# Two query blocks of an attention in turns, and the numbers by which a planner places the other work

## The chip, the cores and the metric

The kernel runs on one core of a Trainium2 chip. Its time is the device time of one execution in microseconds (us); a kernel is told by the median of its runs. Five engines work side by side, each through its own queue in order: TensorE (PE) multiplies matrices, VectorE (DVE) and ScalarE (ACT) work on whole tiles, SyncE (SP) issues nearly all DMA transfers here, and GpSimd (POOL) does nothing of weight.

## The reference

```python
scores = (1.0 / S) * np.matmul(z, z.transpose(0, 2, 1))      # z: (4, 3072, 64)
attn = np.maximum(scores, 0.0) ** 2
x = u * np.matmul(attn, v)                                   # u, v: (4, 3072, 256)
x_prev = np.concatenate([zeros, x[:, :-1, :]], axis=1)
xk = mu_k * x + (1.0 - mu_k) * x_prev
xr = mu_r * x + (1.0 - mu_r) * x_prev
k = np.maximum(xk @ w_k, 0.0)                                # w_k: (256, 1024)
y = 1.0 / (1.0 + np.exp(-(xr @ w_r))) * (k * k @ w_v)
return (np.maximum(y @ w_in, 0.0) ** 2) @ w_out              # w_in: (256, 2048), w_out: (2048, 256)
```

The weights come as 64-bit numbers. Every product is made of three: each operand is split into a rounded part (hi) and its rest (lo), and hi·hi, lo·hi and hi·lo are added up.

## The kernel before

The program has two parts: the attention (with the conversion of the weights beside it), and then the channel mix and the two-layer network, which the change leaves as they are.

**Steps.** Each of the 4 batches has 6 query blocks of 512; the 24 blocks are numbered n, and ib is a block's number within its batch. A block needs 24 steps, one for each chunk of 128 keys, in 6 groups g of 4 chunks. So there are 576 steps s, and `chunk(s)` says which block, group and chunk a step has. The main loop issues, for each s, first what the planner placed there, then `scores(s + 4)`, then `attend(s)`. `attend` is 6 matmuls (L371 and L372 with the hi part of the squared scores, L375 with their lo part). `scores` has three cases:
- g equal to ib ("diagonal"): two matmuls (L343, L344) into PSUM, relu (L157) and square (L158) on ACT, the hi part by DVE (L350), and one step later the lo part by DVE (L353).
- g above ib ("off"): the same, but ACT makes the hi part in two of three steps (L348), and DVE transposes the squared scores (L314, tile `turn`, two buffers). After 4 chunks the tile is stored to DRAM (L318, `turned`). The table `spread` picks the form: for ib of 2 and above the store's layout is "spread", and the transpose takes longer.
- g below ib ("turned"): the scores are the transposed ones of an earlier block. No matmul: `mixed` is loaded from `turned` (L328 or L330), ACT makes hi (L338) and DVE lo (L339).

So a diagonal or off step has 8 matmuls, a turned one 6. Block 0 of a batch has 4 diagonal and 20 off steps, block 5 has 20 turned and 4 diagonal ones, which come first.

**What else lies in the steps.** Each group of z must be turned (`z_turn` L256, DVE), split (`z_hi` L263 on ACT, `z_lo` L266 on DVE) and each group of v split (`prep_v`: L280 on ACT, L278 on DVE). At a block's end the two halves of the result are multiplied by u (`gate` L380, after `prep_u` L290) and stored (L381). The 64-bit weights are converted in 25 pieces of 8 DVE operations each (L119 to L143; 18 more for rests), `conversions`.

**The planner.** Each such piece of work has a cost, an earliest step e and a due step l. The planner goes through the steps with a running balance of the DVE time that a step leaves (`time_left`), puts the piece that is due first into a step when there is room, and at its due step in any case. Conversions get an even spacing over a list of steps `free`. `place` then puts the loads some steps ahead of their use. `EARLY` is how many steps ahead the transposed scores are loaded.

**Queue and buffers.** SP issues in the order in which the code emits. A v load and a weight load (both L91) use the same pool `raw` of 3 buffers; either waits in SP until DVE and ACT have read the buffer's last content, and all that stands behind it in SP waits too.

Of the kernel before, what the change touches and what calls it, by code (L numbers as in the profile page):

```python
# [7 lines left out]
F32 = mybir.dt.float32  # L8
F32R = mybir.dt.float32r
# [6 lines left out]
P = 128  # L16
Q = 32
T = 512
# [3 lines left out]
def tile_relu2_attention__rwkv_channel_mix__relu2_mlp(  # L22
# [18 lines left out]
    nc = tc.nc  # L41
# [5 lines left out]
    NJ = S // P  # L47
    NB = S // T
    NBLK = B * NB
# [5 lines left out]
    G = 4  # L55
    NG = NJ // G
# [20 lines left out]
    spread = {(i, j): i >= 2 for j in range(NB) for i in range(j)}  # L77
# [114 lines left out]
    def acc_tiles(pool=ps_v):  # L192
        return [pool.tile([P, T], F32, tag=f"v{d}", name=f"v{d}") for d in range(ND)]
# [38 lines left out]
    def attention():  # L232
        with ExitStack() as st:
            zp = st.enter_context(tc.tile_pool(name="zp", bufs=1))
            io = st.enter_context(tc.tile_pool(name="io", bufs=2))
            pools["cv"] = st.enter_context(tc.tile_pool(name="cv", bufs=1))
            ps_a = st.enter_context(tc.tile_pool(name="ps_a", bufs=1, space=PSUM))
            ps_w = st.enter_context(tc.tile_pool(name="ps_s", bufs=4, space=PSUM))
            LEAD = 4
# [3 lines left out]
            def load_turned(t, p, src, engine=nc.sync):  # L243

                engine.dma_start(out=t[p:p + Q].rearrange("q (k r) -> q k r", r=Q),
                                 in_=src.rearrange("(k q) r -> q k r", q=Q))

            def load_z(b, g, engines=(nc.sync, nc.sync)):
                z_raw[b, g] = t = io.tile([DQ, T], F32, tag="zn", name="zn")
                for p, e in zip(range(0, DQ, Q), engines, strict=True):  # L250
                    load_turned(t, p, z[b, g * T:(g + 1) * T, p:p + Q], e)


            def z_turn(b, g):
# [37 lines left out]
            at, acc, ready, staged, late = {}, {}, {}, {}, []  # L292
# [2 lines left out]

            def chunk(s):

                n, jc = divmod(s, NJ)  # L300
                if n % NB == NB - 1:
                    jc = (jc - G) % NJ
                return n, n // NB, n % NB, jc // G, jc % G

# [54 lines left out]

            def attend(s):
                n, b, ib, g, c = chunk(s)
                first, last = s % NJ == 0, s % NJ == NJ - 1
                if first:
                    acc[n] = acc_tiles(ps_a if n % 2 else ps_v)
                hi, lo = at.pop(s)
                vt = vhl[b, g]
                for d in range(ND):
                    ds_ = slice(d * P, (d + 1) * P)  # L370
                    nc.tensor.matmul(acc[n][d], lhsT=vt[:, 0, c, ds_], rhs=hi, start=first, stop=False)  # L371
                    nc.tensor.matmul(acc[n][d], lhsT=vt[:, 1, c, ds_], rhs=hi, start=False, stop=False)  # L372
                for d in range(ND):
                    ds_ = slice(d * P, (d + 1) * P)
                    nc.tensor.matmul(acc[n][d], lhsT=vt[:, 0, c, ds_], rhs=lo, start=False, stop=last)  # L375
# [10 lines left out]
            def at_step(s, f, *a):  # L386
                todo.setdefault(s, []).append((f, a))

            n_steps = NBLK * NJ
            for n in range(NBLK):  # L390
                for d in range(ND):
                    at_step(n * NJ + NJ, gate, n, d)

            freed, taken, EARLY = [], 0, 30
            for n in range(NBLK - 1):
                b, ib = divmod(n, NB)
                for g in range(ib):
                    need, stored = n * NJ + (g + ib // (NB - 1)) * G - LEAD, (b * NB + g) * NJ + ib * G + G - 1 - LEAD
# [28 lines left out]
            def time_left(t):  # L427
                if t >= n_steps:
                    return 0.5
                n, _, ib, g, _ = chunk(t)  # L430
                left = 0.72 if g < ib else 0.85 if g == ib else 0.05 if spread[ib, g] else 0.4
                return left - (0.6 if t % NJ in (LEAD, LEAD + 1) and t > NJ else 0)

            first_of = lambda b, g: b * NB * NJ + G * g
            chains, loads = [], []
            for b in range(B):
                z_chain, v_chain = [], []
                chains += [z_chain, v_chain]
                for g in range(NG):
                    i = g | 1  # L440
                    e = first_of(b - 1, 0) + (i * NJ + (NJ if i < NB - 1 else G)) - LEAD if b else -LEAD
                    l = min(first_of(b, g) if not b else first_of(b, 0) - 3 * (NG - g), first_of(b, g)) - LEAD - 2
                    if b or g > 1:
# [3 lines left out]
                    e = first_of(b - 1, 0) + (NB - 1) * NJ + G * min(g + 2, NG) if b else max(-LEAD + 1, G * g - 8)  # L447
                    l = e + (9 if g == NG - 1 else 3) if b else first_of(b, g) - 3
                    v_chain += [(0.2 + 0.4 * lo, prep_v, (b, g, h, lo), e, l + h * 2 + lo) for h in range(2) for lo in range(2)]
            for n in range(NBLK):  # L450
                for d in range(ND):
                    chains.append([(0.65, prep_u, (n, d), n * NJ + 4, n * NJ + 14 + 4 * d)])
            free = [t for t in range(NJ, n_steps - NJ) if chunk(t + LEAD)[2] < NB - 1 and time_left(t + LEAD) > 0.2]
            total = sum(8 + rests for _, _, rests in conversions)
            k0 = 0
            converting = []
# [21 lines left out]
            def place(load, use, last_use, bufs, ahead):  # L478
                ts = sorted((t, a[:2]) for (f, a), t in when.items() if (f, a[2:]) == use)
                done = sorted(t for (f, a), t in when.items() if (f, a[2:]) == last_use)  # L480
                for i, (t, a) in enumerate(ts):
                    s = max(t - ahead, done[i - bufs] + 1 if i >= bufs else -LEAD, -LEAD)
                    assert s < t or t < 0, (a, s, t)
                    if (load, a) != (load_v, (0, 0)):
                        todo.setdefault(s, []).insert(0, (load, a))

            place(load_z, (z_turn, ()), (z_turn, ()), 2, 8)
            place(load_u, (prep_u, ()), (prep_u, ()), 2, 8)
            place(load_v, (prep_v, (0, 0)), (prep_v, (1, 1)), 3, 8)

            s = n_steps - NJ
# [15 lines left out]

            at_step(2 * NJ, load_mu)
            at_step(3 * NJ, lambda: nc.vector.tensor_scalar(out=om, in0=mu, scalar1=-1.0, scalar2=1.0, op0=ALU.mult, op1=ALU.add))
            for g in range(2):  # L510
                load_z(0, g, (nc.sync, nc.scalar))
            load_v(0, 0)
            for g in range(2):
                z_turn(0, g)
                for first in (True, False):
                    z_hi(0, g, first)
                    z_lo(0, g, first)
            for s in range(-LEAD, n_steps + 1):
                for f, a in todo.pop(s, ()):
                    f(*a)  # L520
# [124 lines left out]
    with tc.manual_schedule():  # L645
        attention()
        channel_mix_and_mlp()
# [29 lines left out]
```

## Time and profile before

| | us |
|---|---|
| median of 3 runs (lowest to highest) | 2620.96 (2620.56 to 2626.17) |
| the profiled execution | 2623.58 |
| its span in the trace | 2621.8 |
| PE, DVE, ACT busy in the span | 2584.5, 1762.7, 1516.5 |
| attention part, to the first change of pace | 0 to about 1003.6 |

The profiled execution lies 2.62 us above the median and 1.78 us above its own span. PE's granted clock over the whole run is 0.998 of full. Line numbers are those of the kernel before; in the changed kernel L343 to L381 stand 4 lines further down (L375 becomes L379, L314 becomes L318), while L91, L256, L263, L266, L278, L280 and L290 stay.

### The profile page before, as it was taken

How to read it: one execution, taken by the hardware profiler on the slowest of the kernel's cores; microseconds unless marked ns; L12 is line 12 of the kernel's file. 1: busy time of each engine (PE TensorE's matmuls, PEld its weight loads, DVE VectorE, ACT ScalarE, POOL GpSimd, SP SyncE). 2: the span in 40 equal slices, each digit the busy share in tenths (PEclk: the TensorE clock that was granted, in tenths of full speed). 3: DMA queues.
4: the chain of work that ended last, by engine and by line, in shares of the span. 5: the costliest groups of instructions: out<-in, count | busy, mean ns of one | idle time of the engine just before them, and what ended most of it. 6: DMA issues, size and time to landing. Idle time of an engine off the chain costs nothing.

```text
span 2621.8 us, 32181 instructions
## 1 busy us (share of the span) xinstructions
PE 2584.5 (99%) x11328; PEld 2128.0 (81%) x11328; DVE 1762.7 (67%) x3074; ACT 1516.5 (58%) x2527; POOL 0.2 (0%) x4
## 2 busy tenths in 40 slices
PE   7999999999999999999999999999999999999998
PEld 5888788878788788888888888888888888888887
DVE  7898898898889886655555555555555555555554
ACT  7766876776687665554455545445444554455544
POOL 0000000000000000000000000000000000000000
PEclk9999999999999999999999999999999999999999
DMA  6667667577767761000000000000000000000000
GB/s 164 177 183 191 186 189 193 170 229 194 187 215 193 197 177 65 17 17 17 17 17 17 17 14 11 17 17 17 13 12 17 17 17 17 17 17 17 17 9 17
DMA packets 275602, 215.51 MB, mean 82 GB/s; under 512 B 185072, under 2 KB 203504, under 8 KB 272368
## 3 DMA queue, kind: packets, MB, share of 16 engines
q1 hardware_dynamic: 273328, 213.06, 30.6%
q8 instruction: 88, 1.44, 0.2%
q10 hardware_dynamic: 2112, 0.39, 0.1%
q14 instruction: 74, 0.61, 0.1%
HBM read 121.13 MB, written 92.27 MB: 81 GB/s over the span
## 4 chain that ended last, share of the span: by engine, by line
PE 91%; DVE 2%; DMA 2%; ACT 2%; issue 1%; SPq 1%; DVEq 0%; ACTq 0%
PE ups L203 32%; PE v L375 8%; PE v L372 8%; PE v L371 8%; PE o L564 7%; PE o L565 7%; PE o L568 7%; PE v L219 3%; PE v L218 3%; PE v L222 3%; PE sps L344 2%; PE sps L343 2%; DMA turned<-turn 1%; DMA xT<-uT 1%; DVE alo L353 1%
## 5 line engine op out<-in xcount | busy, mean ns | idle before, releaser
L157 ACT ACTIVATE a<-ups 128x512 f32<-128x512 f32 x576 | 344.1, 597 | 758.5 <-PE ups L203 742.7
L84 DVE CAST hhi<-a 128x512 fp32r<-128x512 f32 x568 | 241.9, 426 | 620.3 <-ACT a L158 603.0
L158 ACT ACTIVATE a<-a 128x512 f32<-128x512 f32 x912 | 576.8, 632 | 29.1
L203 PE MATMUL ups<-x,win 128*128 128x512 f32 x2304 | 584.7, 389 | 0.5 <-DVE x L84 0.5
L203 PEld LDWEIGHTS ups<-x,win 128*128 128x128 f32 x2304 | 432.4, 188 | 90.7 <-DVE x L84 0.9
L372 PE MATMUL v<-ahi,vhl 128*128 128x512 f32 x1152 | 451.1, 392 | 9.9 <-DVE vhl L278 9.9
L371 PE MATMUL v<-ahi,vhl 128*128 128x512 f32 x1152 | 450.0, 391 | 0.9 <-DVE ahi L350 0.9
L85 DVE TENSOR_TENSOR hlo<-a,hhi 128x512 fp32r<-128x512 f32 x568 | 393.5, 693 | 53.1 <-DVE hhi L84 0.9
L375 PE MATMUL v<-alo,vhl 128*128 128x512 f32 x1152 | 358.4, 392 | 11.5 <-DVE alo L339 5.9
L564 PE MATMUL o<-hhi,wout 128*128 128x512 f32 x768 | 298.8, 389 | 0.0
L565 PE MATMUL o<-hhi,wout 128*128 128x512 f32 x768 | 298.8, 389 | 0.0
L203 PE MATMUL ups<-mixed,wk 128*128 128x512 f32 x1152 | 292.1, 389 | 0.0
L375 PEld LDWEIGHTS v<-alo,vhl 128*128 128x128 f32 x1152 | 215.3, 188 | 64.0 <-DVE alo L353 10.8
L372 PEld LDWEIGHTS v<-ahi,vhl 128*128 128x128 f32 x1152 | 217.3, 189 | 58.5 <-DVE vhl L278 13.2
L371 PEld LDWEIGHTS v<-ahi,vhl 128*128 128x128 f32 x1152 | 217.1, 188 | 46.7 <-issue 1.6
L203 PEld LDWEIGHTS ups<-mixed,wk 128*128 128x128 f32 x1152 | 216.2, 188 | 44.9
L157 ACT ACTIVATE a<-sps 128x512 f32<-128x512 f32 x336 | 199.7, 594 | 89.0 <-PE sps L344 82.5
L568 PE MATMUL o<-hlo,wout 128*128 128x512 f32 x768 | 236.4, 389 | 0.0
L314 DVE STREAM_TRANSPOSE turn<-a 128x512 f32<-128x512 f32 x240 | 206.8, 862 | 29.3 <-ACT a L158 14.0
L353 DVE TENSOR_TENSOR alo<-a,ahi 128x512 fp32r<-128x512 f32 x336 | 220.9, 659 | 0.0
L338 ACT CAST ahi<-mixed 128x512 fp32r<-128x512 f32 x220 | 130.6, 618 | 123.9 <-PE v L372 59.4
L565 PEld LDWEIGHTS o<-hhi,wout 128*128 128x128 f32 x768 | 144.2, 188 | 30.0
(70 smaller groups left out, 2558.5 us busy)
## 6 DMA issues: line engine op xcount, KB each, us to landing
turned<-turn SPq DMA_DIRECT2D x60, 1024.0 KB, 4.8
mixed<-turned SPq DMA_DIRECT2D x220, 256.0 KB, 5.1
raw<-in_v_dram SPq DMA_DIRECT2D x24, 512.0 KB, 4.4
u<-in_u_dram SPq DMA_DIRECT2D x192, 64.0 KB, 4.2
xT<-uT SPq DMA_DIRECT2D x48, 256.0 KB, 3.8
out_dram<-y SPq DMA_DIRECT2D x94, 128.0 KB, 2.9
x<-xT SPq DMA_DIRECT2D x20, 513.0 KB, 3.8
zz<-turned SPq DMA_DIRECT2D x20, 256.0 KB, 4.6
```

Source lines behind the costliest of these rows:

```text
L84: nc.vector.tensor_copy(hi, src)
L85: nc.vector.tensor_tensor(out=lo, in0=src, in1=hi, op=ALU.subtract)
L157: nc.scalar.activation(out=a, in_=ps, func=AF.Relu, scale=scale)
L158: nc.scalar.activation(out=a, in_=a, func=AF.Square)
L203: nc.tensor.matmul(ps, lhsT=lhs(h, c, f), rhs=rhs[:, m, c, :], start=k == 0, stop=k == 3 * ND - 1)
L353: finish(lambda: nc.vector.tensor_tensor(out=lo, in0=a, in1=hi, op=ALU.subtract))
L371: nc.tensor.matmul(acc[n][d], lhsT=vt[:, 0, c, ds_], rhs=hi, start=first, stop=False)
L372: nc.tensor.matmul(acc[n][d], lhsT=vt[:, 1, c, ds_], rhs=hi, start=False, stop=False)
L375: nc.tensor.matmul(acc[n][d], lhsT=vt[:, 0, c, ds_], rhs=lo, start=False, stop=last)
L564: nc.tensor.matmul(acc_o[n][d], lhsT=w[:, 0, c, ds_], rhs=hi, start=f == 0, stop=False)
L565: nc.tensor.matmul(acc_o[n][d], lhsT=w[:, 1, c, ds_], rhs=hi, start=False, stop=False)
L568: nc.tensor.matmul(acc_o[n][d], lhsT=w[:, 0, c, ds_], rhs=lo, start=False, stop=f == NF2 - 1)
```

## The change

Blocks 0 and 1 of the first batch are worked in turns, a group of the one and a group of the other (list `order`); all later blocks keep their order. `first`, `last`, the gates and all due steps are rewritten with `pos` and `end`. The planner's numbers change: what a step leaves, where conversions may stand (from block 2 on in place of block 1, filter 0.1 in place of 0.2), earliest and due steps of v and z, and how far ahead u, z and the transposed scores are loaded. Only the first z group is loaded and split ahead of the loop, and ten matmuls of zeros are issued ahead of the first scores.

```diff
+            order = [(0, 0)] + [(n, g) for g in range(1, NG) for n in range(2)] + [(1, 0)]
+            order += [(n, (g - (n % NB == NB - 1)) % NG) for n in range(2, NBLK) for g in range(NG)]
+            pos = {ng: i * G for i, ng in enumerate(order)}
+            end = [max(pos[n, g] for g in range(NG)) + G for n in range(NBLK)]
...
-                n, jc = divmod(s, NJ)
-                if n % NB == NB - 1:
-                    jc = (jc - G) % NJ
-                return n, n // NB, n % NB, jc // G, jc % G
+                n, g = order[s // G]
+                return n, n // NB, n % NB, g, s % G
...
-            freed, taken, EARLY = [], 0, 30
+            freed, taken, EARLY = [], 0, 36
...
-                left = 0.72 if g < ib else 0.85 if g == ib else 0.05 if spread[ib, g] else 0.4
-                return left - (0.6 if t % NJ in (LEAD, LEAD + 1) and t > NJ else 0)
+                left = 0.72 if g < ib else 0.8 if g == ib else 0 if spread[ib, g] else 0.15
+                return left - (0.6 if t - LEAD in end or t - LEAD - 1 in end else 0)
...
-            free = [t for t in range(NJ, n_steps - NJ) if chunk(t + LEAD)[2] < NB - 1 and time_left(t + LEAD) > 0.2]
+            free = [t for t in range(2 * NJ, n_steps - NJ) if chunk(t + LEAD)[2] < NB - 1 and time_left(t + LEAD) > 0.1]
...
-            place(load_z, (z_turn, ()), (z_turn, ()), 2, 8)
-            place(load_u, (prep_u, ()), (prep_u, ()), 2, 8)
+            place(load_z, (z_turn, ()), (z_turn, ()), 2, 12)
+            place(load_u, (prep_u, ()), (prep_u, ()), 2, 14)
...
-            for g in range(2):
-                load_z(0, g, (nc.sync, nc.scalar))
+            load_z(0, 0, (nc.sync, nc.scalar))
             load_v(0, 0)
-            for g in range(2):
-                z_turn(0, g)
-                for first in (True, False):
-                    z_hi(0, g, first)
-                    z_lo(0, g, first)
+            load_z(0, 1, (nc.scalar, nc.scalar))
+
+            t = io.tile([P, T], F32R, tag="ahi", name="zeros", bufs=LEAD + 1)
+            nc.vector.memset(t.bitcast(F32), 0.0)
+            ps = ps_w.tile([P, T], F32, tag="w", name="warm")
+            for i in range(10):
+                nc.tensor.matmul(ps, lhsT=t[:, 0:P], rhs=t, start=True, stop=True)
+            z_turn(0, 0)
+            for first in (True, False):
+                z_hi(0, 0, first)
+                z_lo(0, 0, first)
```

What the planner makes of it is read from the order of the instructions on each engine. Three places matter.

**The start, DVE.** Before, both z groups (`zT` from `zn`, `zz`) are made ahead of the first hi part (`ahi`):

```order
L256 STREAM_TRANSPOSE zT_124<-zn_116 64x512
L266 TENSOR_TENSOR zz_126<-zT_124,zz_126 64x512 x2
L256 STREAM_TRANSPOSE zT_131<-zn_119 64x512
L266 TENSOR_TENSOR zz_126<-zT_131,zz_126 64x512 x2
L256 STREAM_TRANSPOSE zT_145<-zn_142 64x512
L350 CAST ahi_153<-a_150 128x512
L350 CAST ahi_168<-a_165 128x512
L353 TENSOR_TENSOR alo_154<-a_150,ahi_153 128x512
L278 TENSOR_TENSOR vhl_158<-raw_122,vhl_158 128x512
```

Now the second z group comes behind the first hi part, and its last rest (the second `zz` from `zT_158`) only behind the third hi part and the second v rest (`vhl`):

```order
L266 TENSOR_TENSOR zz_139<-zT_137,zz_139 64x512 x2
L354 CAST ahi_155<-a_152 128x512
L256 STREAM_TRANSPOSE zT_158<-zn_121 64x512
L266 TENSOR_TENSOR zz_139<-zT_158,zz_139 64x512
L278 TENSOR_TENSOR vhl_163<-raw_119,vhl_163 128x512
L354 CAST ahi_172<-a_169 128x512
L357 TENSOR_TENSOR alo_156<-a_152,ahi_155 128x512
L354 CAST ahi_186<-a_183 128x512
L357 TENSOR_TENSOR alo_173<-a_169,ahi_172 128x512
L278 TENSOR_TENSOR vhl_163<-raw_119,vhl_163 128x512
L266 TENSOR_TENSOR zz_139<-zT_158,zz_139 64x512
```

That last row is what the fifth pair of score matmuls waits for, and in PE's queue the first `attend` stands behind that pair, before and now.

**The start of the fourth batch, SP.** Here `turned0_1` is the store of the first transposed group of the batch, `raw` a v or weight load, `u` the load of u in four parts. Before, only the two stores of the last block's result (`xT2`) and a v load stand ahead of it:

```order
L91 DMA raw_7384<-in_v_dram 128x4x256
L422 DMA w_out32_79<-m_6934 128x2x256
L91 DMA raw_7469<-in_v_dram 128x4x256
L381 DMA xT2_82<-uT_7192 128x512
L381 DMA xT2_82<-uT_7220 128x512
L318 DMA turned0_1_84<-turn_7484 128x4x512
L330 DMA mixed_7550<-turned0_1_84 32x4x512
```

Now a weight load, then a v load that takes over a buffer, and a u load stand ahead of it:

```order
L91 DMA raw_7434<-in_moe2_w_out_dram 128x2x512
L245 DMA u_7452<-in_u_dram 32x16x32 x4
L385 DMA xT2_82<-uT_7313 128x512
L385 DMA xT2_82<-uT_7363 128x512
L91 DMA raw_7519<-in_v_dram 128x4x256
L245 DMA u_7538<-in_u_dram 32x16x32 x4
L322 DMA turned0_1_84<-turn_7490 128x4x512
```

The v load `raw_7519` waits for DVE's last read of `raw_7415`. On DVE of the changed kernel that read (the first L278 here) stands two rows ahead of the first transpose of the third group, which takes the buffer of `turned0_1`'s store:

```order
L318 STREAM_TRANSPOSE turn_7576<-a_7626 128x16x32
L357 TENSOR_TENSOR alo_7610<-a_7606,ahi_7609 128x512
L278 TENSOR_TENSOR vhl_7565<-raw_7415,vhl_7565 128x512
L128 SCALAR_TENSOR_TENSOR e_7114<-raw_6775,e_7114 128x512
L318 STREAM_TRANSPOSE turn_7652<-a_7646 128x16x32
L357 TENSOR_TENSOR alo_7630<-a_7626,ahi_7629 128x512
```

So the store can only be issued after that L278, and the transpose two rows later waits until it has landed. The third batch has the same sequence now (v load, u load, store), and in the second batch a weight load alone stands in the store's way.

**The last steps of a spread stretch, DVE** (block 14, chunks 20 to 23). Before, one conversion (L143) and no turn of u stand in this place:

```order
L143 TENSOR_TENSOR m_6049<-m_6049,e_5981 128x512
L350 CAST ahi_6223<-a_6220 128x512
L314 STREAM_TRANSPOSE turn_6226<-a_6220 128x16x32
L353 TENSOR_TENSOR alo_6204<-a_6200,ahi_6203 128x512
L314 STREAM_TRANSPOSE turn_6226<-a_6239 128x16x32
L353 TENSOR_TENSOR alo_6224<-a_6220,ahi_6223 128x512
L314 STREAM_TRANSPOSE turn_6226<-a_6256 128x16x32
```

Now two conversions (L119, L122) and a turn of u (L290) stand there:

```order
L119 TENSOR_SCALAR e_6215<-raw_5886 128x512
L354 CAST ahi_6223<-a_6220 128x512
L318 STREAM_TRANSPOSE turn_6226<-a_6220 128x16x32
L357 TENSOR_TENSOR alo_6204<-a_6200,ahi_6203 128x512
L290 STREAM_TRANSPOSE uT_6236<-u_5978 128x512
L122 TENSOR_SCALAR e_6215<-e_6215 128x512
L318 STREAM_TRANSPOSE turn_6226<-a_6242 128x16x32
L357 TENSOR_TENSOR alo_6224<-a_6220,ahi_6223 128x512
```

Over the 12 spread steps of this block the order has 3 conversions and no turn of u before, 7 conversions and 2 turns of u now. Over all spread off steps it has 13 conversions before and 51 now; beside the other off steps 55 and 56, beside diagonal steps 53 and 50, beside turned steps 97 and 61.

## Rows read from the trace of the kernel before

**Rows 1.** The page's busy times: engine, busy us, share of the span, instructions.

```profile
PE 2584.5 (99%) x11328; PEld 2128.0 (81%) x11328; DVE 1762.7 (67%) x3074; ACT 1516.5 (58%) x2527; POOL 0.2 (0%) x4
```

**Rows 2.** Windows: stretch, us, busy us (count) of PE, PEld, DVE, ACT, POOL; clock, DMA.

```profile
0.00:111.80 111.80, 94.09 (x376) 73.23 (x377) 88.57 (x154) 85.53 (x146) 0.20 (x4) 0.97 0.63 172
264.60:310.00 45.40, 43.36 (x186) 34.02 (x186) 38.05 (x69) 36.70 (x63) 0.00 (x0) 1.00 0.67 202
504.00:550.70 46.70, 43.34 (x185) 34.07 (x184) 37.98 (x69) 35.68 (x61) 0.00 (x0) 1.00 0.68 202
747.20:788.90 41.70, 41.70 (x185) 34.53 (x185) 37.95 (x69) 35.52 (x61) 0.00 (x0) 1.00 0.75 227
```

**Rows 3.** The chain that ended last, a stretch in the network: start, us, what.

```profile
1020.33 2.72 PE ups L203 x12
```

**Rows 4.** Timeline of DVE, the start: start, us, instruction, count [idle before <-releaser].

```profile
3.82 0.70 DVE L256 STREAM_TRANSPOSE zT<-zn 64x512 f32<-64x512 f32 x1 [3.82 <-DMA zn<-in_z_dram]
```

**Rows 5.** Timeline of ACT, the start.

```profile
7.44 1.26 ACT L263 CAST zz<-zT 64x512 fp32r<-64x512 f32 x2 [1.62 <-DVE zT L256]
8.72 0.60 ACT L157 ACTIVATE a<-sps 128x512 f32<-128x512 f32 x1
9.35 0.63 ACT L158 ACTIVATE a<-a 128x512 f32<-128x512 f32 x1
```

**Rows 6.** Timeline of PE, the start.

```profile
6.76 0.77 PE L344 MATMUL sps<-zz 128*128 128x512 f32 x1
7.32 0.63 PE L343 MATMUL sps<-zz 128*128 128x512 f32 x1
7.75 0.63 PE L344 MATMUL sps<-zz 128*128 128x512 f32 x1
...
18.05 0.47 PE L371 MATMUL v<-ahi,vhl 128*128 128x512 f32 x1
```

**Rows 7.** Timeline of SP, first block of the third batch.

```profile
516.94 0.37 SPq L91 DMA_DIRECT2D raw<-in_v_dram  x1
...
518.38 0.46 SPq L318 DMA_DIRECT2D turned<-turn  x1
525.24 0.32 SPq L330 DMA_DIRECT2D mixed<-turned  x1
525.60 2.03 SPq L245 DMA_DIRECT2D u<-in_u_dram  x4
```

**Rows 8.** Timeline of DVE there: the third and fourth transposed groups begin.

```profile
525.32 0.71 DVE L314 STREAM_TRANSPOSE turn<-a 128x512 f32<-128x512 f32 x1 [5.08 <-DMA turned<-turn]
...
534.17 0.71 DVE L314 STREAM_TRANSPOSE turn<-a 128x512 f32<-128x512 f32 x1 [2.12 <-DMA turned<-turn]
```

**Rows 9.** The page's DMA issues: count, KB each, median us from issue to landing.

```profile
turned<-turn SPq DMA_DIRECT2D x60, 1024.0 KB, 4.8
```

**Rows 10.** Timeline of DVE, the end of block 14's spread stretch.

```profile
621.47 0.71 DVE L143 TENSOR_TENSOR m<-m,e 128x512 f32<-128x512 f32 x1
622.07 0.45 DVE L350 CAST ahi<-a 128x512 fp32r<-128x512 f32 x1
622.40 1.12 DVE L314 STREAM_TRANSPOSE turn<-a 128x512 f32<-128x512 f32 x1
623.43 0.67 DVE L353 TENSOR_TENSOR alo<-a,ahi 128x512 fp32r<-128x512 f32 x1
624.00 1.12 DVE L314 STREAM_TRANSPOSE turn<-a 128x512 f32<-128x512 f32 x1
...
628.52 1.27 DVE L353 TENSOR_TENSOR alo<-a,ahi 128x512 fp32r<-128x512 f32 x2
```

**Rows 11.** Timeline of PE there: the lo products of block 14's last chunk but one.

```profile
630.03 0.62 PE L375 MATMUL v<-alo,vhl 128*128 128x512 f32 x2
```

**Rows 12.** Waits of PE from 112 to 1003 us: engine, line, waited for, us, times, longest.

```profile
PE v L375 <- DVE alo L339: 5.9, 6, 1.9
```

More of the change, by code (lines that the diff above doesn't have):

```diff
@@ L363, in attend @@
                 n, b, ib, g, c = chunk(s)
-                first, last = s % NJ == 0, s % NJ == NJ - 1
+                first, last = n not in acc, s + 1 == end[n]
                 if first:
@@ L391, in attention @@
                 for d in range(ND):
-                    at_step(n * NJ + NJ, gate, n, d)
-            freed, taken, EARLY = [], 0, 30
+                    at_step(end[n], gate, n, d)
+            freed, taken, EARLY = [], 0, 36
             for n in range(NBLK - 1):
@@ L397, in attention @@
                 for g in range(ib):
-                    need, stored = n * NJ + (g + ib // (NB - 1)) * G - LEAD, (b * NB + g) * NJ + ib * G + G - 1 - LEAD
+                    need, stored = pos[n, g] - LEAD, pos[b * NB + g, ib] + G - 1 - LEAD
                     s = max(need - EARLY, stored + 1, freed[-4] if len(freed) > 3 else 0, taken)
@@ L430, in time_left @@
                 n, _, ib, g, _ = chunk(t)
-                left = 0.72 if g < ib else 0.85 if g == ib else 0.05 if spread[ib, g] else 0.4
-                return left - (0.6 if t % NJ in (LEAD, LEAD + 1) and t > NJ else 0)
-            first_of = lambda b, g: b * NB * NJ + G * g
-            chains, loads = [], []
+                left = 0.72 if g < ib else 0.8 if g == ib else 0 if spread[ib, g] else 0.15
+                return left - (0.6 if t - LEAD in end or t - LEAD - 1 in end else 0)
+            chains = []
             for b in range(B):
                 z_chain, v_chain = [], []
-                chains += [z_chain, v_chain]
+                chains += [v_chain, z_chain]
+                n0 = b * NB
                 for g in range(NG):
[L440 to L443, printed above, removed]
+                    if b:
+                        n = n0 - NB + (g | 1)
+                        e, l = (end[n] if g < NB - 2 else pos[n, NB - 1] + G) - LEAD, end[n0 - 1] - 3 * (NG - g) - LEAD - 2
+                    else:
+                        e, l = max(1 - LEAD, pos[0, g] - LEAD - 9), pos[0, g] - LEAD - (3 if g > 1 else 1)
+                    if b or g:
                         z_chain += [(0.65, z_turn, (b, g), e, l - 5), (0, z_hi, (b, g, True), e, l - 4),
@@ L446, in attention @@
                                     (0.6, z_lo, (b, g, False), e, l)]
-                    e = first_of(b - 1, 0) + (NB - 1) * NJ + G * min(g + 2, NG) if b else max(-LEAD + 1, G * g - 8)
-                    l = e + (9 if g == NG - 1 else 3) if b else first_of(b, g) - 3
-                    v_chain += [(0.2 + 0.4 * lo, prep_v, (b, g, h, lo), e, l + h * 2 + lo) for h in range(2) for lo in range(2)]
+                    if b:
+                        e = end[n0 - 1] - G * max(NG - 2 - g, 0)
+                        l = e + (10 if g == NG - 1 else 4)
+                    else:
+                        e, l = max(1 - LEAD, pos[0, g] - 10), pos[0, g] - 5
+                    v_chain += [(0.2 + 0.4 * lo, prep_v, (b, g, h, lo), e, l + h * 3 + lo) for h in range(2) for lo in range(2)]
             for n in range(NBLK):
                 for d in range(ND):
-                    chains.append([(0.65, prep_u, (n, d), n * NJ + 4, n * NJ + 14 + 4 * d)])
-            free = [t for t in range(NJ, n_steps - NJ) if chunk(t + LEAD)[2] < NB - 1 and time_left(t + LEAD) > 0.2]
+                    e = (end[n - 1] if n else 0) + 3
+                    chains.append([(0.65, prep_u, (n, d), e, min(e + 10 + 4 * d, end[n] - 4 + d))])
+            free = [t for t in range(2 * NJ, n_steps - NJ) if chunk(t + LEAD)[2] < NB - 1 and time_left(t + LEAD) > 0.1]
             total = sum(8 + rests for _, _, rests in conversions)
@@ L483, in place @@
                     assert s < t or t < 0, (a, s, t)
-                    if (load, a) != (load_v, (0, 0)):
+                    if (load, a) != (load_v, (0, 0)) and (load, a) != (load_z, (0, 1)):
                         todo.setdefault(s, []).insert(0, (load, a))
-            place(load_z, (z_turn, ()), (z_turn, ()), 2, 8)
-            place(load_u, (prep_u, ()), (prep_u, ()), 2, 8)
+            place(load_z, (z_turn, ()), (z_turn, ()), 2, 12)
+            place(load_u, (prep_u, ()), (prep_u, ()), 2, 14)
             place(load_v, (prep_v, (0, 0)), (prep_v, (1, 1)), 3, 8)
```

## The prediction

> **What bounds the kernel now.** First the page: PE is busy in 99% of the span [rows 1], so a change can win only what PE still waits, and lose by making it wait more. What a matmul costs when nothing waits is read from the chain: twelve in 2.72 us, 0.2267 us each [rows 3]. A diagonal or off step (8 matmuls) is then 1.81 us, a turned one (6) 1.36 us. The windows show where PE falls behind that pace. The first two blocks have 376 matmuls, 85.2 us at full pace, and take 111.8 us: 26.6 us are lost [rows 2]. The first block of each later batch has 185 or 186 matmuls and takes 41.7 us in the fourth batch, 45.4 in the second, 46.7 in the third: 3.7 and 5.0 us lost, and none [rows 2]. In the rest of the attention PE's longest list of waits is for lo parts of turned steps, 5.9 us in 6 waits [rows 12]. The network behind it runs at pace, isn't touched, and counts at nothing.
>
> **The start and the two blocks in turns.** Before, attend of the second chunk begins at 18.05, with 18 matmuls done [rows 6]. I follow the chain by hand with the new order. The second score product ends at 7.53 (6.76 + 0.77) [rows 6]. ACT's relu, which stood behind the two casts of the second z group until 8.72 [rows 5], can go then: relu 0.62, square 0.63, so DVE's hi part is made at 9.1. Now the second z group begins: turn to 9.8 (0.70 [rows 4]), two casts to 11.1 (1.26 [rows 5]), one v cast to 11.6 (taken as the CASTs). Relu and square of the second chunk end at 12.9, and of the third, with another v cast between, at 14.6. DVE then has a hi part (0.33), a lo part (0.57), a v rest (0.6) and the last z rest (0.7): 16.8. The fifth pair of score products and the first attend follow at the pace of the first ones, 0.43 us from start to start [rows 6], eight of them: 20.2, and the next pair brings attend of the second chunk to 20.6, 2.6 us later than before. From there 376 - 18 = 358 matmuls are left, and z and v groups are wanted only every eighth step in place of every fourth, so I let PE run at pace: 81.2 us, end at 101.8 in place of 111.8. That is **-10.0 us**. Bounds: -7, since ACT has 85.5 us of work in these blocks [rows 2] against PE's 85.2 and may cost some 3 us, and -12.5, if the start is no later than before.
>
> The ten products of zeros cost at most 4.3 us at 0.43. They need only the memset, and DVE is idle until 3.82 and PE until the first score product behind it [rows 4]; without that cover a late memset would delay the scores by what is left of the 4.3. I take 0. No row shows PE busy from the start, so what the clock does then isn't seen: the rows show 0.43 us from start to start for the early scores, twice the 0.2267, that is 1.2 GHz in place of 2.4, after an idle start.
>
> The Trainium skill, page "TensorE: Matmul & The Clock Gate", section "Part 1: The HAM clock gate (the "warmup" mystery)", says that the array is throttled by default and that activity releases it. By that rule the zeros might release the first scores: two products at 0.23 in place of 0.43 would bring the relu some 0.4 to 0.9 us forward, and the sum would be -10.9 in place of -10.0.
>
> I keep 0, since the following wait of PE (from the fourth score pair to 16.8) gives the clock time to fall again.
>
> **The starts of the later batches.** Here a store holds DVE. In the third batch the v load goes out at 516.94, the store of the first transposed group at 518.38, it has landed at 525.24 (6.86 us) [rows 7], and only then DVE goes on with the third group, after 5.08 us idle; the fourth waits 2.12 us more [rows 8]. Of these 7.2 us PE loses 5.0 [rows 2], so 2.2 us of a stall are covered by the lead of four steps. In the changed order of the third and the fourth batch the v load waits for DVE's last v rest, and behind it in SP stand the u load and the store; on DVE there is one operation (0.60) until the transpose that needs the store's buffer. Counted from that rest: v load 0.42 (516.94 and the next issue), u load 2.1 (2.03 and a gap), landing 6.86 [rows 7], less 0.6: DVE stands 8.8 us. The fourth group waits less than before, because the u load is already through: I take 0.7. PE loses 8.8 + 0.7 - 2.2 = 7.3 us, twice, 14.6 against 5.0 + 0. In the second batch only a weight load stands between: 0.42 + 6.86 - 0.33 + 0.7 - 2.2 = 5.5 against 3.7. Together **+11.4 us**. Low bound: all landings at the median of 4.8 us [rows 9] and no second stall, 4.5 + 4.5 + 2.7 against 8.7: +3. High bound: the second stall at 2.1 again, 8.7 + 8.7 + 6.9 against 8.7: +15.6.
>
> **Conversions beside spread steps.** The new order puts 51 conversion operations beside spread steps, 13 before. On DVE a spread step takes a transpose 1.03 (622.40 to 623.43) and a lo part 0.57 (to 624.00), and in one step of three a hi part 0.33 (622.07 to 622.40) [rows 10]: 1.71 us of PE's 1.81. Twelve such steps leave 1.3 us. In block 14 the old order puts 3 conversions there, 0.33 + 0.6 + 0.6 = 1.5 us (the 0.6 from 621.47 to 622.07 [rows 10]). The new one puts 7 (four of 0.33, three of 0.6: 3.1 us) and two turns of u at 0.63: 4.4 us, 3.1 too much. Added up step by step in the same way, DVE's arrears at the end of the stretch are 1.0 before and 3.1 after. In the trace of before the lo part of the last chunk but one ends about 629.18 (the first of the two from 628.52 [rows 10]), and its products begin at 630.03 [rows 11]: 0.85 us spare with arrears of 1.0. With 2.1 more, PE waits 2.1 - 0.85 = 1.25 us. Eight stretches end with arrears of 2.7 to 3.9: 8 x 1.25 = +10.0. Against it, u is loaded earlier, and so in places no longer ahead of the transposed scores in SP: of the 5.9 us of waits on turned lo parts [rows 12] I let 2.5 go. **+7.5 us**, with bounds 0 (DVE makes good its arrears unseen and the loads gain as much as it loses) and +13 (no load gains, three more ends wait). Everything else that moves (z turns, v rests, loads ahead by 12, 14 and 36 steps) is the same work in other steps.
>
> **Sum.** -10.0 + 11.4 + 7.5 = +8.9 us. The profiled execution of before, 2623.58, would become 2632.5; it lies 2.6 above the median, so against the median of 2620.96 I get 2629.9, put at 2630.
>
> **The rivals.**
> - *The store isn't held.* If the v load's buffer is free early (DVE runs ahead of PE by its lead), store and transposes keep the pace that the fourth batch has before, where PE loses nothing [rows 2]. Then the starts give 8.7 us back: -10.0 - 8.7 + 7.5 = -11.2, 2609.8. For it speaks that row; against it that the v rest itself stands two rows ahead of the waiting transpose. It decides where the landing comes within 2.2 us of DVE's need.
> - *The arrears don't reach PE.* DVE is idle in a third of the span, and diagonal and turned steps leave it time; were the stretches' ends covered and the loads still gain 2.5, then -10.0 + 11.4 - 2.5 = -1.1: 2619.9, no change. Against it speak the 0.85 us spare [rows 10, 11].
> - *The turns don't do what they are said to.* ACT has as much to do as PE in the first two blocks [rows 2]; were they to win only 3 us, the sum is +15.9: 2636.9.
> - *Cheap landings*, the low bound of the starts: -10.0 + 3 + 7.5 = +0.5: 2621.5, no change.
>
> **Numbers.** Chances: the forecast 0.47 (its own range 2626 to 2637), the store not held 0.20, the arrears not seen 0.12, the turns winning little 0.11, cheap landings 0.10. A measurement here tells 0.2% (5.2 us) from no change, that is 2615.7 to 2626.2. The first rival is faster; of the second and the last nearly all is same, and a little of the forecast too; the rest is slower. The range runs from the first rival's time, which half of its chance exceeds, to beyond the third: 2609 to 2643.
>
> **What would show it.** The first two blocks end near 102 us, with attend of the second chunk near 20.6. In the first blocks of the third and fourth batch DVE's transpose stands idle 8 to 9 us behind the turned store, with the v and u load just ahead of that store in SP. At the ends of spread stretches PE waits 1 to 2 us for lo parts of L357 (L353 before). The prediction is wrong if DVE's idle time before those transposes stays under 3 us, or if PE shows no waits at the stretches' ends.

## The result, and the profile after

The changed kernel takes 2651.11 us (median of 4 runs, 2648.49 to 2653.92), the kernel before 2621.6 beside it: a ratio of 1.0109, 95% interval 1.0091 to 1.0127. It is slower by 29.5 us, where 9 were forecast, and lies 8 us above the range.

The page of the changed kernel, its busy times and its chain of waits by engine:

```profile
PE 2599.6 (98%) x11338; PEld 2131.9 (80%) x11338; DVE 1763.0 (66%) x3073; ACT 1516.7 (57%) x2529; POOL 0.2 (0%) x4
...
PE 74%; DVE 7%; DMA 5%; issue 2%; SPq 2%; ACT 1%; DVEq 0%; ACTq 0%
```

Against [rows 1] DVE and ACT have no more to do. PE has ten instructions more, the zeros (4.27 us), and is busy 15.1 us longer; the rest of that is the same matmuls, taking longer. What is new stands in the chain: DVE and DMA are 12% of it, 4% before. To see where, cut the attention at the first attend of blocks 2, 6, 7, 12, 13, 18 and 19 and of block 22's last group. This gives the first two blocks, then in turns a long stretch of four or five blocks and the first block (the "start") of the next batch. Windows of the changed kernel (columns as in [rows 2]):

```profile
0.00:103.56 103.56, 94.14 (x386) 75.32 (x387) 81.83 (x141) 86.24 (x147) 0.20 (x4) 0.95 0.70 188
103.56:257.12 153.56, 152.37 (x668) 124.55 (x666) 131.87 (x220) 103.28 (x177) 0.00 (x0) 1.00 0.68 175
257.12:306.38 49.26, 44.69 (x185) 36.39 (x184) 39.82 (x73) 36.98 (x64) 0.00 (x0) 0.93 0.68 198
306.38:508.34 201.96, 197.45 (x850) 159.05 (x848) 169.80 (x289) 136.46 (x233) 0.00 (x0) 0.99 0.67 175
508.34:566.51 58.17, 44.86 (x185) 35.12 (x184) 40.03 (x73) 36.73 (x63) 0.00 (x0) 0.94 0.59 171
566.51:764.70 198.19, 195.80 (x850) 157.87 (x848) 171.99 (x296) 134.00 (x228) 0.00 (x0) 1.00 0.74 193
764.70:817.74 53.04, 45.44 (x186) 35.90 (x184) 40.05 (x73) 36.70 (x63) 0.00 (x0) 0.94 0.62 188
817.74:970.83 153.09, 152.05 (x665) 124.17 (x664) 130.07 (x226) 102.94 (x173) 0.00 (x0) 1.00 0.73 191
```

The same cuts for the kernel before have lengths 111.81, 152.83, 45.34, 194.05, 46.67, 196.54, 41.71 and 152.91. In the fifth experiment below, where next to nothing waits, the four long stretches take 150.96, 194.50, 192.21 and 150.51, and each start 41.7. These lengths are the pace, but for the 194.50, for which I take the 192.21 of the first experiment. So, lost against the pace:

| stretch | before | changed | difference | forecast |
|---|---|---|---|---|
| first two blocks, their length | 111.81 | 103.56 | -8.3 | -10.0 |
| start of the second batch | 3.6 | 7.6 | +3.9 | +1.8 |
| start of the third | 5.0 | 16.5 | +11.5 | +2.3 |
| start of the fourth | 0 | 11.3 | +11.3 | +7.3 |
| the four long stretches | 10.4 | 20.9 | +10.5 | +7.5 |
| sum | | | +29.0 | +8.9 |

The sum is 970.83 - 941.86, and nearly all of the 30.3 us between the two spans. The three starts hold 15.3 of the 20.1 us between this sum and the forecast, those of the third and the fourth batch 13.2.

There DVE's stalls are those that were forecast. DVE of the changed kernel at the transposes that wait for the store, third batch and fourth:

```profile
539.96 0.71 DVE L318 STREAM_TRANSPOSE turn<-a 128x512 f32<-128x512 f32 x1 [8.18 <-DMA turned<-turn]
...
790.58 0.71 DVE L318 STREAM_TRANSPOSE turn<-a 128x512 f32<-128x512 f32 x1 [7.96 <-DMA turned<-turn]
```

8.18 and 7.96 us, forecast 8.8; in the second batch it is 6.59, forecast 6.95. SP of the third batch shows the chain, and something else:

```profile
510.93 0.37 SPq L91 DMA_DIRECT2D raw<-in_moe_w_in_dram  x1
517.74 0.37 SPq L91 DMA_DIRECT2D raw<-in_v_dram  x1
...
531.50 0.38 SPq L91 DMA_DIRECT2D raw<-in_v_dram  x1
531.93 2.52 SPq L245 DMA_DIRECT2D u<-in_u_dram  x4
534.50 1.02 SPq L322 DMA_DIRECT2D turned<-turn  x1
539.88 0.79 SPq L334 DMA_DIRECT2D mixed<-turned  x2
```

The second half is the hold as forecast: v load 531.50, u load, store 534.50, landed before 539.88. But the v load before it, at 517.74, was late too: a weight load had taken a buffer at 510.93, and this v load waited for DVE. ACT of that stretch:

```profile
522.12 0.62 ACT L280 CAST vhl<-raw 128x512 fp32r<-128x512 f32 x1 [5.70 <-DMA raw<-in_v_dram]
```

The v cast stands in ACT's queue ahead of the next relu, so ACT's 5.70 us became 6.24 of DVE's and 3.50 of PE's, before the forecast stall began. PE of the two starts, with its idle time:

```profile
525.60 0.73 PE L379 MATMUL v<-alo,vhl 128*128 128x512 f32 x2 [3.50 <-DVE alo L357]
526.17 0.39 PE L347 MATMUL sps<-zz 128*128 128x512 f32 x1
526.40 0.40 PE L348 MATMUL sps<-zz 128*128 128x512 f32 x1
...
541.30 1.22 PE L379 MATMUL v<-alo,vhl 128*128 128x512 f32 x2 [8.12 <-DVE alo L357]
...
791.91 1.22 PE L379 MATMUL v<-alo,vhl 128*128 128x512 f32 x2 [6.20 <-DVE alo L357]
792.93 0.63 PE L347 MATMUL sps<-zz 128*128 128x512 f32 x1
```

In the fourth batch PE loses 6.20 of DVE's 7.96 us. In the third it loses 8.12 of 8.18: the lead of four steps was used up by the gap of 3.50 us before.

And a long gap can cost more than itself. Windows around that of 6.20 us:

```profile
786.00:792.00 6.00, 0.09 (x1) 0.09 (x1) 1.42 (x3) 1.79 (x4) 0.00 (x0) 0.85 0.79 220
792.00:798.00 6.00, 6.00 (x16) 4.76 (x17) 5.48 (x11) 4.80 (x9) 0.00 (x0) 0.58 0.88 288
```

After it the granted clock is 0.58: 16 matmuls in 6 us, where 26 fit; that is 6 - 16 x 0.2267 = 2.4 us on top of the gap.

### The profile page after: what moved, and what is told of

Read it like the earlier page. It is cut to its first block, busy times and chain, and to the rows that moved or that the text cites. A ratio compares the mean times of both kernels' runs of the same rounds, so it can differ in the third digit from the quotient of the medians.

```text
span 2652.1 us, 32190 instructions
## 1 busy us (share of the span) xinstructions
PE 2599.6 (98%) x11338; PEld 2131.9 (80%) x11338; DVE 1763.0 (66%) x3073; ACT 1516.7 (57%) x2529; POOL 0.2 (0%) x4
## 4 chain that ended last, share of the span: by engine, by line
PE 74%; DVE 7%; DMA 5%; issue 2%; SPq 2%; ACT 1%; DVEq 0%; ACTq 0%
PE ups L203 32%; PE o L581 7%; PE o L580 7%; PE o L584 7%; PE v L379 4%; PE v L375 4%; PE v L376 4%; PE v L218 3%; PE v L222 3%; PE v L219 3%; DVE alo L357 2%; DMA mixed<-turned 2%; DMA turned<-turn 2%; DVE turn L318 2%; PE sps L348 1%
## 5 line engine op out<-in xcount | busy, mean ns | idle before, releaser
L343 DVE TENSOR_TENSOR alo<-mixed,ahi 128x512 fp32r<-128x512 f32 x220 | 144.9, 690 | 51.5 <-ACT ahi L342 48.1
```

## The experiments

A theory of mine, in two parts, and two rivals stood against each other. Mine: stores held behind v and weight loads cost the starts, and DVE's arrears from conversions beside spread steps cost the rest. First rival: the loads that go out further ahead (12, 14, 36) crowd SP. Second rival: the turns, or the new due steps of z and v, cost it.

**Old numbers for what a step leaves** (e1_old_time_left), in the changed kernel:

```diff
-                left = 0.72 if g < ib else 0.8 if g == ib else 0 if spread[ib, g] else 0.15
+                left = 0.72 if g < ib else 0.85 if g == ib else 0.05 if spread[ib, g] else 0.4
...
-            free = [t for t in range(2 * NJ, n_steps - NJ) if chunk(t + LEAD)[2] < NB - 1 and time_left(t + LEAD) > 0.1]
+            free = [t for t in range(2 * NJ, n_steps - NJ) if chunk(t + LEAD)[2] < NB - 1 and time_left(t + LEAD) > 0.2]
```

> The changed kernel with the old numbers for what a step leaves (0.85, 0.05, 0.4) and the old filter of 0.2 for the conversions; all else as changed. The order has 13 conversion operations beside spread steps again, and the store of the second batch is no longer held; those of the third and fourth still stand behind the v load and the u load. Theory (held stores and DVE's arrears): the arrears at the stretches' ends, 10.6 us, and the second batch's 7.6 us go, the other two starts stay: about 2633 us. Rival (the loads that are issued further ahead crowd SP, whatever the conversions do): no change from 2651. Second rival (the turns and the new due steps of z and v cost it): no change either.

Measured 2621.01 against 2622.82, ratio 0.9994 (0.9984 to 1.0003). Windows of this run, from the second batch's start to the fourth's:

```profile
254.21:295.91 41.70, 41.70 (x185) 34.54 (x184) 38.56 (x70) 36.03 (x62) 0.00 (x0) 1.00 0.82 231
295.91:488.12 192.21, 192.21 (x849) 159.21 (x848) 170.34 (x291) 138.31 (x233) 0.00 (x0) 1.00 0.69 182
488.12:542.52 54.40, 45.40 (x186) 36.00 (x184) 39.09 (x71) 36.68 (x63) 0.00 (x0) 0.94 0.67 193
542.52:734.76 192.24, 192.24 (x849) 159.18 (x848) 172.88 (x299) 135.30 (x228) 0.00 (x0) 1.00 0.74 196
734.76:789.18 54.42, 45.10 (x185) 35.64 (x184) 39.09 (x71) 36.69 (x63) 0.00 (x0) 0.94 0.60 184
```

The new numbers for what a step leaves, with their filter, cost 30 us in the changed kernel. As expected the second batch's start is clean and the third's and fourth's still lose 12.7 each. The miss of 12 us is on the good side: between the starts nothing is lost at all, where I had let only the 10.6 us at the stretches' ends go. So the loads ahead crowd nothing: with them PE runs at pace.

**Pieces shared out over the batches** (e2_aligned), in the changed kernel. Each batch gets its own list of steps, which leaves out the first ones of a later batch:

```diff
+            for b, m in enumerate((4, 7, 7, 7)):
+                mine = conversions[i0:i0 + m]
+                own = [t for t in free if (t + LEAD) // (NB * NJ) == b and (not b or (t + LEAD) % (NB * NJ) >= 20)]
+                many, k0 = sum(8 + rests for _, _, rests in mine), 0
...
-                steps = [free[(k0 + k) * len(free) // total] for k in range(8 + rests)]
+                    steps = [own[(k0 + k) * len(own) // many] for k in range(8 + rests)]
```

> The changed kernel with all its numbers, but the 25 pieces are shared out over the batches (4, 7, 7, 7), so that no piece is begun before a batch's last block and ended in the next batch: no weight load stands at the starts of batches 2 to 4 until their own v loads are out. 62 conversion operations stand beside spread steps (51 in the changed kernel). Theory: the three starts, 35 us together, fall to 5 or less, the arrears stay or grow by 2: about 2621 us. Rival (loads further ahead crowd SP): the u load still stands ahead of the store, so 2645 or more. Second rival (turns and due steps): 2651.

Measured 2624.53 against 2622.82, ratio 1.0008 (0.9999 to 1.0018), so 26.6 us less than the changed kernel. Windows of its second batch's start and of what follows:

```profile
262.06:303.76 41.70, 41.70 (x185) 34.53 (x184) 37.18 (x65) 36.11 (x63) 0.00 (x0) 1.00 0.73 223
303.76:503.99 200.23, 195.77 (x850) 157.83 (x848) 174.71 (x302) 136.39 (x233) 0.00 (x0) 1.00 0.71 184
```

All three starts take 41.7 us, though the u load still stands ahead of the store in SP: what held the store is the v load that waits for a buffer. The edit also takes conversions off DVE there (65 DVE instructions in the second batch's start, 73 in the changed kernel). Two rows speak against these as the cause: in the changed kernel DVE stands idle 6.59 us at this place, and e1's clean start of the second batch has 70. The long stretches lose more than in the changed kernel, 28.1 us together against 20.9 (in the one shown 200.23 - 192.21 = 8.0), with 62 conversion operations beside spread steps. The two costs are separate.

**The turns with all other numbers of before** (e3_turns_old_numbers): e1's edit and

```diff
-            freed, taken, EARLY = [], 0, 36
+            freed, taken, EARLY = [], 0, 30
...
-            free = [t for t in range(2 * NJ, n_steps - NJ) if chunk(t + LEAD)[2] < NB - 1 and time_left(t + LEAD) > 0.2]
+            free = [t for t in range(NJ, n_steps - NJ) if chunk(t + LEAD)[2] < NB - 1 and time_left(t + LEAD) > 0.2]
...
-            place(load_z, (z_turn, ()), (z_turn, ()), 2, 12)
-            place(load_u, (prep_u, ()), (prep_u, ()), 2, 14)
+            place(load_z, (z_turn, ()), (z_turn, ()), 2, 8)
+            place(load_u, (prep_u, ()), (prep_u, ()), 2, 8)
```

> The two blocks in turns with their new due steps and the new start, but all other numbers of before: what a step leaves, filter, conversions from block 1 on, loads 8, 8 and 30 steps ahead. In its order the store of the second batch stands behind a weight load and that of the third behind a v load, with no u load ahead of either; that of the fourth is free. Theory: 8 us from the first two blocks, starts about as before (8.7) or 4 worse: 2614 to 2618 us. Rival (loads ahead): the same, so this run can't tell these two apart. Second rival (turns and due steps cost it): 2640 or more.

Measured 2642.59 against 2622.82, ratio 1.008 (1.0065 to 1.0095). This is the second rival's number, and mine is missed by 25 us. Windows of the second and the third batch's start:

```profile
264.10:314.32 50.22, 44.65 (x185) 35.27 (x184) 38.34 (x69) 37.23 (x64) 0.00 (x0) 0.97 0.66 193
...
508.92:564.48 55.56, 46.08 (x185) 36.58 (x184) 38.28 (x70) 36.73 (x62) 0.00 (x0) 0.91 0.57 171
```

They lose 8.5 and 13.9 us, 3.6 and 5.0 before. In the third batch DVE stands 7.44 us for the first store and 4.64 more for a later one, before which a weight load had again waited in SP. Whether the turns and their due steps do this by themselves, or by way of the pieces that hold a buffer, the next run tells.

**The same with the pieces shared out** (e4_turns_aligned): e3's and e2's edits.

> As the kernel with the turns and the numbers of before, and with the pieces shared out over the batches (4, 7, 7, 7). 24 conversion operations stand beside spread steps; the stores of all three starts go out when their data are ready. Theory: 8 us from the first two blocks and the 8.7 us that the starts lose before, less 1 to 3 for more arrears: 2605 to 2609 us. Rival (loads ahead): the pieces don't matter, 2614 to 2618. Second rival (turns and due steps): 2640 or more.

Measured 2611.01 against 2622.82, ratio 0.9953 (0.9936 to 0.9969): 31.6 us less than e3. Its three starts take 41.7 us each. The starts make 24.7 of the 31.6 us. So the turns and the new due steps do no harm at the starts by themselves; with pieces across the batch's start they do. The time is 2 us above what I expected: the long stretches lose 12.7 us, 10.4 before.

**Turns, loads ahead, shared-out pieces, old numbers for what a step leaves** (e5_loads_and_aligned): e1's and e2's edits, and conversions from block 1 on.

> The turns, the new loads ahead (12, 14, 36), the old numbers for what a step leaves with conversions from block 1 on, and the pieces shared out over the batches (4, 7, 7, 7). Theory: as the first experiment (2621), whose losses lay in the starts of the third and fourth batch alone, 25.5 us, without these and with 1 us for more conversions beside spread steps: 2595 to 2600 us. Rival (the starts wait for the u load, which still stands ahead of the store, not for the weight pieces): 2610 or more.

Measured 2598.3 against 2620.73, ratio 0.9916 (0.9901 to 0.9931): faster than both kernels, by 22 and 53 us. Windows:

```profile
0.00:103.15 103.15, 93.34 (x387) 74.23 (x387) 86.18 (x150) 86.50 (x148) 0.20 (x4) 0.97 0.72 193
103.15:254.11 150.96, 150.96 (x668) 125.00 (x666) 132.61 (x220) 105.33 (x177) 0.00 (x0) 1.00 0.70 180
254.11:295.81 41.70, 41.70 (x185) 34.53 (x184) 38.09 (x69) 35.99 (x62) 0.00 (x0) 1.00 0.78 232
295.81:490.31 194.50, 193.40 (x849) 158.78 (x848) 173.87 (x297) 137.16 (x233) 0.00 (x0) 1.00 0.72 187
490.31:532.02 41.71, 41.71 (x185) 34.55 (x184) 38.17 (x69) 36.14 (x63) 0.00 (x0) 1.00 0.81 229
532.02:724.23 192.21, 192.21 (x849) 159.21 (x848) 170.86 (x293) 135.37 (x228) 0.00 (x0) 1.00 0.73 197
724.23:765.94 41.71, 41.71 (x185) 34.55 (x184) 38.17 (x69) 36.14 (x63) 0.00 (x0) 1.00 0.82 230
765.94:916.45 150.51, 150.51 (x666) 124.67 (x664) 132.39 (x229) 103.90 (x173) 0.00 (x0) 1.00 0.74 199
```

PE's busy time is the whole stretch in six of the eight rows. What is left of the attention's losses is the first two blocks' start, about 18 us, and 2.3 us in the long stretch behind the second batch's start.

**The kernel before with shared-out pieces** (e6_before_aligned): e2's edit in the kernel before.

> The kernel before, nothing changed but the pieces shared out over the batches (4, 7, 7, 7). Theory: the 8.7 us that the second and third batch lose at their starts go, 1 to 2 come for more conversions beside spread steps: 2614 to 2617 us. Rival (the starts wait for something else): as before, 2622.

Measured 2615.07 against 2620.73, ratio 0.9976 (0.9966 to 0.9986). The starts of the second and third batch, which lost 8.6 us before, take 41.71 each; the long stretches lose some 11 us, as before.

**Without the products of zeros** (e7_no_zeros), in the changed kernel:

```diff
-            t = io.tile([P, T], F32R, tag="ahi", name="zeros", bufs=LEAD + 1)
-            nc.vector.memset(t.bitcast(F32), 0.0)
-            ps = ps_w.tile([P, T], F32, tag="w", name="warm")
-            for i in range(10):
-                nc.tensor.matmul(ps, lhsT=t[:, 0:P], rhs=t, start=True, stop=True)
```

> The changed kernel without the ten products of zeros and their memset. Theory: the start is set by ACT and DVE, so within 1 us of the changed kernel's 2651. Rival (the zeros bring PE's clock up for the first scores): 1 to 4.5 us slower.

Measured 2654.37 (2651.63 to 2655.68) against 2620.73; its span, 2651.9 us, is within 0.2 of the changed kernel's 2652.1. The medians are 3.3 us apart, more than the 1 us I expected, but the runs overlap, so the time decides nothing. The rows do. PE of the changed kernel, with the zeros:

```profile
1.44 4.27 PE L529 MATMUL warm<-zeros 128*128 128x512 f32 x10 [1.44 <-DVE zeros L526]
...
6.80 0.40 PE L347 MATMUL sps<-zz 128*128 128x512 f32 x1
7.03 0.39 PE L348 MATMUL sps<-zz 128*128 128x512 f32 x1
...
16.50 0.77 PE L348 MATMUL sps<-zz 128*128 128x512 f32 x1 [5.24 <-DVE zz L266]
17.06 0.63 PE L375 MATMUL v<-ahi,vhl 128*128 128x512 f32 x1
```

PE without them:

```profile
6.93 0.63 PE L347 MATMUL sps<-zz 128*128 128x512 f32 x1
7.36 0.63 PE L348 MATMUL sps<-zz 128*128 128x512 f32 x1
...
17.23 0.63 PE L375 MATMUL v<-ahi,vhl 128*128 128x512 f32 x1
```

The zeros bring the early scores to 0.23 us from start to start, 0.43 without. (The profile's granted clock reads 1.00 there in both runs, so the spacing alone shows it.) But the first attend comes at 17.06 against 17.23, and at 0.43 in both, after 5 us in which PE was idle. The first two blocks, cut as above, take 103.56 us with the zeros and 102.84 without: they save nothing there.

**The kernel before with the loads ahead** (e8_before_loads): z 12, u 14, transposed scores 36, nothing else.

> The kernel before with the loads ahead of the changed kernel (z 12, u 14, transposed scores 36 steps), nothing else changed. Theory after the first experiment: the late transposed scores, 9.7 us of lost PE time before, vanish, and the starts stay at about 8.7: 2611 to 2615 us. Rival (loads further ahead crowd SP): 2625 or more.

Measured 2611.27 against 2620.73, ratio 0.9964 (0.9952 to 0.9977). The late transposed scores, the row in [rows 12], are gone from PE's list of waits; the two starts lose 2.6 and 5.2.

**The kernel before with both** (e9_before_loads_aligned): what the turns are worth by themselves.

> The kernel before with the loads ahead of the changed kernel and the pieces shared out over the batches: as the fifth experiment, but without the two blocks in turns and without their start. Theory: the gains of the sixth and the eighth experiment lie in different places and add up (5.7 and 9.5 us), about 2605 us, and what is left to the fifth experiment's 2598 is the turns' own gain, 7 to 8 us. Rival (the turns give nothing of their own once the loads are in order): 2598 to 2600.

Measured 2606.87 against 2622.42, ratio 0.9941 (0.9927 to 0.9955). The fifth experiment's median is 8.6 us lower, and so is its span (2605.0 and 2596.4); by the ratios to the runs of before beside each it is 6.6 us. The first two blocks take 111.36 us here and 103.15 there. So the turns and their start are worth about 8 us, as the changed kernel's first row says.

**More products of zeros** (e10_more_zeros): e5 and, at step 0, between the fourth and the fifth pair of score products,

```diff
+            def more_zeros():
+                ps = ps_a.tile([P, T], F32, tag="v0", name="v0")
+                for i in range(34):
+                    nc.tensor.matmul(ps, lhsT=t[:, 0:P], rhs=t, start=True, stop=True)
...
+            at_step(0, more_zeros)
```

> The fifth experiment with 34 more products of zeros between the fourth and the fifth pair of score products, where PE stands idle for about 8 us and its clock falls to half. Theory (the clock falls for want of work): the first attends run at 0.23 us from start to start in place of 0.43, their start stays at 17, so 1 to 1.5 us are won: 2597 us, hardly to be told from 2598 in the time, but to be seen in the rows. Rival (the start's pace is set by ACT and DVE alone): no change in the rows of the second chunk.

Measured 2598.67 against 2622.42, ratio 0.9909 (0.9895 to 0.9922), not to be told from e5. PE:

```profile
8.46 7.87 PE L543 MATMUL v<-zeros 128*128 128x512 f32 x34
...
17.04 0.39 PE L375 MATMUL v<-ahi,vhl 128*128 128x512 f32 x1
17.27 0.39 PE L376 MATMUL v<-ahi,vhl 128*128 128x512 f32 x1
```

The first attends now run at 0.23, and that of the second chunk begins at 18.86 in place of 19.87 in e5. The microsecond does not show in the span, 2596.4 us in both. It is kept until an attend at 88.56 (89.68 in e5) and gone by the one at 92.57 (92.56). Between them DVE waits for a transposed store to land:

```profile
88.79 0.71 DVE L318 STREAM_TRANSPOSE turn<-a 128x512 f32<-128x512 f32 x1 [1.32 <-DMA turned<-turn]
```

In e5 the same transpose begins at 88.79 too, after 0.24 us. The store went out 1.1 us earlier in e10 (81.97 and 83.07) and landed no earlier; why, the rows do not tell.

## Why the prediction was wrong

The direction and the places held; the size did not, above all at the starts of the later batches.

**The two blocks in turns:** -10.0 forecast, -8.3 measured. The hand-worked chain came out close: attend of the first chunk at 17.06 and of the second at 20.47, forecast 20.6. Some of that is luck. A pair of score products at 0.43 is 0.86, where 0.4 was added for "the next pair"; but the first product of the fifth pair, counted behind 16.8, was already done at 10.76. The rest of the two blocks loses 2 us more than "at pace", 0.9 of them before 23.14, where the matmuls still run at 0.43 until 22.2. e9 against e5 confirms it: 8.2 by the length of the two blocks. The rival that the turns win only 3 us is out.

**The zeros:** forecast at nothing, and nothing is seen in the end of the start. That the clock would fall again was right (0.43 at 17.06). The page "TensorE: Matmul & The Clock Gate" of the Trainium skill, section "Part 1: The HAM clock gate (the "warmup" mystery)", says that activity releases the array's throttle. The trace agrees: with the zeros ahead the first scores run at 0.23 in place of 0.43. The 0.9 us that I worked out by it came out as 0.17.

**The starts of the later batches:** this is the step that failed, +11.4 forecast, +26.8 measured, beyond its high bound of +15.6. The stall of DVE was sized rightly (6.6, 8.2, 8.0 for 6.95, 8.8, 8.8), and the hold that makes it. What PE pays for it was not: "8.8 + 0.7 - 2.2" has three faults.
- The 2.2 us that the lead of four steps covers hold only for a first gap: in the second batch PE loses 4.57 of DVE's 6.59 us, in the fourth 6.20 of 7.96. In the third I followed only the load just ahead of the store. One v load earlier, the same held buffer stops ACT for 5.70 us; that makes PE 3.8 us late and uses up the lead, and then PE loses 8.12 of 8.18.
- The sum has no term for the clock behind the gap. Counted from the late lo products on, the matmuls at 0.43 cost 2.9, 1.6 and 2.5 us in the three starts.
- Further groups are late again, for which 0.7 us was allowed: in the third batch the last two groups of four steps lose 2.8 us, in the fourth 2.5, in the second nothing.

That a piece which holds a buffer is the cause of it all is shown by e2, e4, e6 and e1's second batch: without it, 41.7.

**Conversions beside spread steps:** +7.5 forecast, +10.5 measured, from two errors that partly cancel. The 1.25 us for each stretch's end was right: the last window of the changed kernel, which holds the ends of blocks 20 and 21, loses 2.58 us, 1.29 each. Seven of the eight ends lose 0.9 to 1.5 us, 8.3 together, for 10.0 forecast. But time is lost in another place too. In the last blocks of the first three batches, which stood at nothing in the sum ("the same work in other steps"), the turned steps lose 1.7, 2.8 and 3.6 us (by the starts of their attends, in groups of four steps). More of the z work lies there: block 11 has 5 turns of z and 11 rests, 3 and 8 in e1. That a balance eaten up by conversions puts it off is how I read the planner; the smaller numbers could do it by themselves, and no run parts the two. On the other side, the loads ahead are worth more than the 2.5 us that I allowed: 9.5 in e8; in the changed kernel one late load stays, in block 10, for 4.4 us. e1 shows both at once: with the old numbers and the new loads nothing is lost between the starts.

**The rivals:** "the store isn't held" holds in none of the three starts. "The arrears don't reach PE" and "cheap landings" are out too; the landing took 5.4 to 6.4 us, where that rival had 4.8.

**What stays open:** why v rests come later with the new numbers and due steps, and so make the hold worse in e3 than before, was not taken apart; e3 changes several due steps at once. Nor is it known why the store in e10 lands no earlier.

## What to carry to other kernels

When loads of different kinds share a pool and a queue in order, look for the piece that keeps a buffer across a phase in which another kind needs them all: here moving it away was worth 6 us alone and 27 to 32 where the planner had made it worse. A change of a planner's numbers is a change of the whole order; test each number by itself, since here one set cost 30 us in the changed kernel, and another of the same diff, the loads ahead, gained 9.5 in the kernel before. And price a stall of TensorE by its gap, by the clock behind it, and by the next stall that the same late work brings.

## What the runs showed of the hardware

The clock behind a gap of PE was the surprise. In the changed kernel, after 6.20 us idle, the next 6 us have a granted clock of 0.58. After 3.50 us idle (at 525.60) the matmuls run at 0.23 us from start to start at once. And in the kernel before, a gap of 1.85 us at 682.92 is followed by matmuls at 0.43 from 684.07 on. The rows of the kernel before:

```profile
682.92 0.73 PE L375 MATMUL v<-alo,vhl 128*128 128x512 f32 x2 [1.85 <-DVE alo L339]
...
684.07 0.63 PE L371 MATMUL v<-ahi,vhl 128*128 128x512 f32 x1
684.50 0.63 PE L372 MATMUL v<-ahi,vhl 128*128 128x512 f32 x1
```

Nor does a longer gap bring a longer slow stretch: in the changed kernel the matmuls stay at 0.43 until 288.4 after 4.57 us idle (to 282.70), but only until 544.5 after 8.12 us (to 541.30). So the length of a gap alone doesn't tell what follows it. Ten products of zeros, 4.27 us, brought the first scores to 2.4 GHz (0.23 us from start to start), and 34 more kept the clock there until real work came. The kernel did not get shorter by it: the first attend waits for a z rest of DVE, with zeros and without, and what e10 won behind it was lost at the landing of a store.
